# A quarter of each copy of value sums moved from ScalarE to VectorE

## The chip, the core and the metric

The kernel runs on one core of a Trainium2 chip. The metric is the device time of one execution in microseconds; lower is better. The engines are named as in the profile: PE is TensorE's matmul and PEld its weight load, DVE is VectorE, ACT is ScalarE, POOL is GpSimd, and SP is the engine that issues the transfers.

## The reference

For 2048 tokens of width 512, the kernel computes self-attention with 32 heads of 16 and a gated layer of width 1792, and mixes the two by a sigmoid gate per token. All numbers are fp32.

```python
qkv = (x @ wqkv).reshape(B, S, 3, H, Dh)              # H = 32, Dh = 16
scores = einsum("bhqd,bhkd->bhqk", q, k) * Dh ** -0.5
a = (softmax(scores) @ v) @ wo                        # heads side by side
b = (sigmoid(x @ w_gate) * (x @ w_up)) @ w_down       # width F = 1792
g = sigmoid((x * gate_w).sum(-1, keepdims=True))
out = g * a + (1 - g) * b
```

## The kernel before

Attention is done for 16 pairs of heads, one after the other. A loop of 256 steps (`for k in range(NPER)`) holds nearly the whole time: 16 steps a pair, each with two tiles of 128 keys against 1024 queries. A step has five kinds of work, all put in order by hand:

- *Scores and exponentials* (`st_part`, words `t0` and `t1` of the order). TensorE multiplies 512 queries with a tile of keys into a PSUM bank, and ScalarE writes the exponential into a tile `p` (L686). Eight a step.
- *Rows of maxima* (`mx` and `sm_step`, words `m0` and `m1`). The softmax needs the largest score of each query. It is found LEAD steps ahead, from score products of their own (L294), which VectorE reduces from the bank (L296). Eight a step, each of 512 columns.
- *The dense layers* (`dense`, words `d0` and `d1`): halves of matmuls that fill the other half of TensorE's rows; ScalarE takes their sums out of the bank `dn` (L609).
- *Value products* (`values`, at the step's end). 16 matmuls (L848) multiply the step's exponentials with the values and add up in one bank, `sm0`. A copy of 128 x 512 takes the bank into a tile, `sum` for the first of eight steps and `part` for the others.
- *Sums of these copies* (`add`). GpSimd adds each `part` to its `sum`; after eight steps the sum goes to HBM. `part` has two buffers.

The seven banks that scores, maxima and value products share are numbered in `seven`, 0 to 3 for `sm0` to `sm3` and 4 to 6 for `st0` to `st2`. The order of a step says after each word which bank it uses:

```python
STEADY = ("m1:3 t0:2 m0:4 d1 d1 t0:5 m0:6 d1 d1 t0:1 d1 m0:3 d1 t0:2 turn m0:0 t1:4 "
          "m1:5 d0 d0 t1:1 t1:6 d0 d0 m1:2 d0 m1:3 t1:4 d0")
SUMS = 0
```

So the maxima of a step use the banks 3, 4, 6, 3, 0, 5, 2 and 3, in that order, and VectorE reduces them in that order too. The fifth of them uses bank 0, `sm0`, as the value products do: these can start only when VectorE has reduced it. For the last 11 steps (`k >= FREE`) there are no maxima any more, and VectorE does the copy of the value sums; before, ScalarE does it (L853), in 245 steps.

VectorE has other work between the last row of maxima of one step and the first of the next, in some steps: the logit of a token tile (`logits`, L835), reciprocals of the denominators (`dens`, L806), and once in eight steps a reduction and a transpose of the gathered maxima (L300, L302). Each engine takes its instructions in the order written; the order of SP's transfers alone is set by the scheduler.

Of the kernel before, what the change touches and what calls it, by code (L numbers as in the profile page):

```python
# [12 lines left out]
F32 = mybir.dt.float32  # L13
F32R = mybir.dt.float32r
AF = mybir.ActivationFunctionType
# [10 lines left out]
P = 128  # L26
# [9 lines left out]
LEAD = 22  # L36
NSTEP = NPAIR * 32
NPER = NSTEP // 2
FREE = NPER - LEAD // 2
EARLY = 5  # L40
WARM = 9
HF = NF // 2
LOW, UP = 0, 1

# [2 lines left out]
def gated_mix(ctx, tc, x, xT, wqk, wv, wo, w_gate, w_up, w_down, gate_w, out):  # L47
    nc = tc.nc
    pe, act, dve, pool, sp = nc.tensor, nc.scalar, nc.vector, nc.gpsimd, nc.sync

    ctx.enter_context(tc.manual_schedule(engines=ORDERED))
    keep = ctx.enter_context(tc.tile_pool(name="keep", bufs=1))
# [31 lines left out]

    for _ in range(WARM):
        pe.matmul(banks[2], z.to_broadcast([P, P]), z.to_broadcast([P, 512]), start=True, stop=True)
# [33 lines left out]
    def raw_cols(src, n, name):  # L120
        return raw_weights(src[n], [P, KT, P], name)
# [57 lines left out]
    later, turnover, slow, soon = [], [], [], []  # L179
# [210 lines left out]
    def filling():  # L390
        pairs = [(m, i) for i in range(HF) for m in range(2)]
        qk = [(2, 0), (3, 0)]
        jobs = [("qk", 1)] + [("far", i) for i in range(HF + 1)]
        for ns in (qk, pairs):
# [4 lines left out]
        def beside(m, i):  # L399
            return i + HF if m < 2 else i + 1  # L400

        def raws(kind, n):
            if kind == "qk":
                return [raw_qk(n, b) for b in range(2)]
            if kind == "far":
                both = []
                for m in range(2):
                    raw = keep.tile([P, KT, P], F32, name=f"far{m}{n}r", tag="wr", bufs=2)
                    sp.dma_start(raw[:, 2:], gu_w[m][n][:, 2:] if n < HF else wqk[2, 1, :, m])
                    both.append(raw)  # L410
# [6 lines left out]
            if m >= 2:  # L417
                return [raw_weights(wqk[f, :, :, m - 2].rearrange("b p k f -> p b k f"), [P, KT, P],
                                    f"{kind}{m}_{f}") for f in (2, 3)]
            return [raw_cols(gu_w[m], i + a, f"{kind}{m}_{i + a}") for a in (0, HF)]  # L420

# [47 lines left out]
        def out_of(run, name):  # L469
            e = keep.tile([P, 512], F32, name=name, tag="er", bufs=6)  # L470
            leave(e, run.o)
            return e

        def place(m, f, c):
            to = gu_d[m, f] if m < 2 else s_d[m - 2, f]
            return to[:, c * 512:(c + 1) * 512]

        def sums_of(kind, n, ws):
# [7 lines left out]
            elif kind == "far":  # L486
                for m in range(2):
                    for c in range(2):
                        run = Sum(bankd(), quarter(ws[m], 2, c))
                        yield run  # L490
                        sp.dma_start(place(m, n, c) if n < HF else place(2 + m, 0, c), out_of(run, f"far{m}{n}_{c}"))
            elif kind == "side":
# [129 lines left out]
    for c in range(NC):  # L622
# [20 lines left out]
        for i, m in order:  # L643
            o, ops, dst = two[i]
# [167 lines left out]
    def split_load(r):  # L812
        f, t, c = r // 8, r // 4 % 2, r % 4
        e = split_in[r] = keep.tile([P, 2, 512], F32R, name=f"sq{r}", tag="ev", bufs=2)
        sp.dma_start(e[:, 0, :].bitcast(F32), s_d[t, f, :, c * 512:(c + 1) * 512])
# [13 lines left out]
    def logit_load(t):  # L829
        tok[t] = keep.tile([P, 2, D], F32, name=f"xn{t}", tag="ev", bufs=2)  # L830
        sp.dma_start(tok[t], x[t * P:(t + 2) * P, :].rearrange("(t p) d -> p t d", p=P))
# [6 lines left out]
    sums = {}  # L838

    def values(k):  # L840

        o = bank()
        half = divmod(k // 8, 2)
        pts = [ptile.pop((k, b)) for b in range(2)]
        for a in range(2):
            for c in reversed(range(4)):
                h = 2 * half[0] + c // 2
                pe.matmul(o[32 * c:32 * c + VW, :], v[:, 2 * k % 16 + a, h * VW:(h + 1) * VW],  # L848
                          pts[c // 2][:, 2 * a + c % 2, :], start=(a == 0), stop=(a == 1))

        def put(e):
            if 2 * k + LEAD < NSTEP:
                act.activation(e, o, AF.Copy)  # L853
            else:
                dve.tensor_copy(e, o)
        if half not in sums:
            sums[half] = keep.tile([P, 512], F32, name=f"sum{half[0]}_{half[1]}", tag="sum", bufs=2)
            put(sums[half])
        else:
            e = keep.tile([P, 512], F32, name=f"part{k}", tag="part", bufs=2)  # L860
            put(e)
            later.append((1.3, lambda s=sums[half]: add(s, e)))

        def add(s, e):
            pool.tensor_tensor(s, s, e, ALU.add)  # L865
            if k % 8 == 7:
                sp.dma_start(pv_d[half[1], half[0]], s)

    def mx(b):
        for j in range(LEAD, NSTEP):  # L870
            one = sm_step(j)
            for i in range(2):
                one(b, i)
                yield
# [5 lines left out]
    def dense(g):  # L880
        while run:
            run.half(g)
            yield
# [20 lines left out]

    parts = {"m0": mx(0), "m1": mx(1), "d0": dense(LOW), "d1": dense(UP)}
    bank = bankm = lambda: spot[0]
    for k in range(NPER):
        n = 2 * k
        if n + LEAD == NSTEP:
            bank = bank7  # L910
            leave = dve.tensor_copy
        if 75 <= k < 123:
            t, r = divmod(k - 75, 6)
            if r in (0, 3):
                split_load(2 * t + r // 3)
            if r in (1, 4):
                split_sum(2 * t + r // 3)
            if r == 1:
                logit_load(2 * t)
            if r in (3, 4):  # L920
                logits(2 * t, r - 3)
        if n % 32 == 0 and n // 32 + 1 < NPAIR:
            load_pair(n // 32 + 1)
        parts["t0"], parts["t1"] = st_part(k, 0), st_part(k + 1, 1) if k + 1 < NPER else iter(())
        emit(BEGIN if k == 0 else STEADY if k < FREE else LAST, **parts)
        if run and run.done():
            run = next(fill, None)
        elif run and run.n:
            turn(run)
        for half in list(mrow):  # L930
            later[:0] = put_max(half)
        work(2.6)
        later.extend(soon)
        soon.clear()
        if k == NPER - 1:
            break
        if NPER - 16 < k <= NPER - 12:
            for _ in range(2):
                next(next(exps))
        spot[:] = [seven[SUMS]]  # L940
        values(k)
        if k == NPER - 17:
            loaded.extend(hidden_load(*chunks[m]) for m in range(2))
            early = [hidden_early(m) for m in range(2)]
            exps = iter([early[0]] * 4 + [early[1]] * 4)
        if 192 <= k < 215 and k % 8 != 4:
            next(dens[0], None)
        if k == NPER - 6:
            next(dens[1])
        if k == NPER - 2:  # L950
            raws = [late_raw(*late[m][:2]) for m in range(2)]
        if k == NPER - 13:
            early = chain(*early)
        if k >= NPER - 13:
            for _ in range(1 if k < FREE else 3):
                next(early, None)
# [72 lines left out]
    for n, (c, f) in enumerate(chunks):  # L1029
        if f == 0:  # L1030
            down = [bankt() for _ in range(4)]
        if n in at:
            heads_out(at[n], heads.pop(at[n]))
        hl = ready[n]
        for t in range(4):
            ops = list(terms([((hl[0][:, a, t * P:(t + 1) * P], hl[1][:, a, t * P:(t + 1) * P]), wd[f + a])
                              for a in range(2)]))
            for m, (a, b) in enumerate(ops):
                pe.matmul(down[t], a, b, start=(f == 0 and m == 0), stop=(f == NF - 2 and m == 5))  # L1039
            if f == NF - 2:  # L1040
                finish(4 * c + t, down[t], g0)
            if (n, t) == (0, 1):
                values(NPER - 1)
                flush(later)
        if n < 3:
            next(dens[1], None)
        if n in (1, 5, 6, 7):
            next(dens[2], None)
        if n + 3 < len(chunks):
            hidden(n + 3)  # L1050
        if n + 2 < len(chunks):
            hidden_split(n + 2)
        if n + 6 < len(chunks):
            loaded.append(hidden_load(*chunks[n + 6]))
        if n == 1:
            xes.close()
            lp = ctx.enter_context(tc.tile_pool(name="lp", bufs=1))
            wd_h = lp.tile([P, NF - 6, D], F32R, name="wd_h")
            wd_l = lp.tile([P, NF - 6, D], F32R, name="wd_l")
            wohl = keep.tile([P, NS * VROW], F32R, name="wohl", tag="va")[:, :2 * KT * D].rearrange(  # L1060
                "p (a k d) -> p a k d", a=2, k=KT)
        late_next()
        if n + 3 in at:
            u = at[n + 3]
            heads[u] = heads_split(u, *heads[u])
        if n + 5 in at:
            u = at[n + 5]
            heads[u] = heads_load(u)
# [25 lines left out]
```

## Time and profile before

| what | value |
| --- | --- |
| median of 3 runs | 1683.34 us (1683.09 to 1683.47) |
| the profiled execution, its own time | 1682.99 us |
| its span (the basis of the shares) | 1681.0 us |
| TensorE matmul busy | 1675.7 us, 100% |
| VectorE busy | 1453.0 us, 86% |
| ScalarE busy | 1360.9 us, 81% |
| GpSimd busy | 942.5 us, 56% |
| granted TensorE clock | full speed, 9 in all 40 slices |

The span is the time between the first and the last instruction of the program on the core. Busy shares are means over all stages. A matmul row includes the short time that it may wait behind its own weight load, so 100% busy doesn't say that TensorE never waits. A row of the timeline is: start, duration, engine, line, operation, output<-inputs, shapes, number of instructions merged into the row, and in brackets the idle time of the engine before it with what ended it.

### The profile page before, as it was taken

Reading aid. Unit: us, or ns where it says so; the run is one execution under the profiler, and the core shown is the slowest. Engines: PE = TensorE matmul, PEld = TensorE weight load, DVE = VectorE, ACT = ScalarE, POOL = GpSimd, SP = SyncE. Lnnn points to the kernel's source line nnn. Section 1 sums busy time; section 2 is a strip of 40 time slices with the busy share of each in tenths; the row PEclk is TensorE's granted clock in tenths of the full one; section 3 lists DMA queues with packets and bytes.
Section 4 is the critical chain, followed back from the end, with each engine's and each line's share of the span. In section 5 each row is a group of like instructions: output and inputs, shape, how many; then the busy total and the mean of one; then the engine's idle time right before and its main releaser. Section 6 shows DMA issues by size and latency. Waiting matters only on the chain.

```text
span 1681.0 us, 34649 instructions
## 1 busy us (share of the span) xinstructions
PE 1675.7 (100%) x12485; PEld 1060.1 (63%) x12485; DVE 1453.0 (86%) x2350; ACT 1360.9 (81%) x2656; POOL 942.5 (56%) x922
## 2 busy tenths in 40 slices
PE   9999999999999999999999999999999999999999
PEld 7766656565656565656565665656565656568887
DVE  7988888888889999999888888889999888887753
ACT  4188888898988898889898989889898989983431
POOL 1134476547656666566666767676666667653110
PEclk9999999999999999999999999999999999999999
DMA  8411447366565564555535353434343434368862
GB/s 271 119 46 59 130 171 211 133 171 206 145 198 136 164 151 154 160 166 188 160 103 146 102 146 108 134 103 133 109 134 105 133 114 158 123 206 277 288 217 70
DMA packets 143788, 254.20 MB, mean 151 GB/s; under 512 B 24256, under 2 KB 36544, under 8 KB 140736
## 3 DMA queue, kind: packets, MB, share of 16 engines
q1 hardware_dynamic: 135024, 235.34, 46.3%
q10 hardware_dynamic: 8592, 16.65, 3.1%
q8 instruction: 98, 1.61, 0.4%
q14 instruction: 74, 0.61, 0.1%
HBM read 149.42 MB, written 102.50 MB: 150 GB/s over the span
## 4 chain that ended last, share of the span: by engine, by line
PE 99%; DVE 0%; DMA 0%; ACT 0%; ACTq 0%; issue 0%; DVEq 0%
PE dn L163 30%; PE sm L848 27%; PE sm L294 16%; PE sm L1039 5%; PE st L684 5%; PE sm L684 5%; PE st L294 2%; PE dn L1039 2%; PE st L1039 2%; PE st L163 2%; PE st L150 1%; PE st L646 1%; PE sm L150 1%; PE st L848 1%; DVE stat L296 0%; DMA x<-in_xT_dram 0%
## 5 line engine op out<-in xcount | busy, mean ns | idle before, releaser
L296 DVE TENSOR_REDUCE stat<-sm 128x1 f32<-128x512 f32 x1314 | 848.2, 681 | 136.6 <-PE sm L684 125.8
L686 ACT ACTIVATE p<-sm 128x512 f32<-128x512 f32 x1030 | 611.0, 630 | 11.3 <-PE st L163 10.1
L686 ACT ACTIVATE p<-st 128x512 f32<-128x512 f32 x1018 | 615.6, 651 | 0.0
L294 PE MATMUL sm<-ks,qs 48*128 48x512 f32 x1314 | 525.2, 435 | 0.0
L848 PE MATMUL sm<-p,v 128*17 128x512 f32 x4016 | 479.9, 595 | 0.0
L296 DVE TENSOR_REDUCE stat<-st 128x1 f32<-128x512 f32 x734 | 478.8, 680 | 0.0
L684 PE MATMUL sm<-qs,ks 64*128 64x512 f32 x1030 | 428.6, 419 | 0.0
L684 PE MATMUL st<-qs,ks 64*128 64x512 f32 x1018 | 425.5, 419 | 0.0
L294 PEld LDWEIGHTS sm<-ks,qs 48*128 48x128 f32 x1314 | 241.0, 184 | 261.7 <-DVE stat L296 214.9
L865 POOL TENSOR_TENSOR sum<-sum,part 128x512 f32<-128x512 f32 x224 | 288.6, 1288 | 135.5 <-PE sm L684 121.7
L294 PE MATMUL st<-ks,qs 48*128 48x512 f32 x734 | 290.0, 395 | 0.0
L848 PEld LDWEIGHTS sm<-p,v 128*17 128x17 f32 x4016 | 93.1, 96 | 224.3 <-issue 155.4
L853 ACT ACTIVATE part<-sm 128x512 f32<-128x512 f32 x214 | 128.3, 600 | 124.1 <-issue 84.1
L544 POOL TENSOR_TENSOR chain<-chain,chain 128x512 f32<-128x512 f32 x96 | 124.3, 1294 | 155.4 <-PE sm L684 140.4
L684 PEld LDWEIGHTS st<-qs,ks 64*128 64x128 f32 x1018 | 187.3, 184 | 29.6 <-issue 3.4
L684 PEld LDWEIGHTS sm<-qs,ks 64*128 64x128 f32 x1030 | 190.0, 185 | 10.5 <-issue 5.1
L544 POOL TENSOR_TENSOR had<-chain,had 128x512 f32<-128x512 f32 x96 | 123.6, 1287 | 39.4 <-PE sm L684 17.8
L294 PEld LDWEIGHTS st<-ks,qs 48*128 48x128 f32 x734 | 137.0, 187 | 1.5 <-ACT v L667 0.5
L609 ACT ACTIVATE chain<-dn 128x512 f32<-128x512 f32 x128 | 88.2, 689 | 0.0
L544 POOL TENSOR_TENSOR side<-side,side 128x512 f32<-128x512 f32 x32 | 41.4, 1294 | 77.9 <-PE sm L684 71.9
L105 POOL TENSOR_TENSOR ol<-ot,oh 128x512 fp32r<-128x512 f32 (+1 forms) x8 | 14.7, 1842 | 102.7 <-ACT oh L102 81.5
L321 POOL CAST mhl<-mt 128x32 fp32r<-128x32 f32 x32 | 7.6, 238 | 101.0 <-DVE mt L302 101.0
(912 smaller groups left out, 3251.5 us busy)
## 6 DMA issues: line engine op xcount, KB each, us to landing
gul<-gu_d SPq DMA_DIRECT2D x56, 512.0 KB
had<-gu_d SPq DMA_DIRECT2D x84, 256.0 KB
gu_d<-had SPq DMA_DIRECT2D x84, 256.0 KB
gu_d<-side SPq DMA_DIRECT2D x56, 256.0 KB
pv_d<-sum SPq DMA_DIRECT2D x32, 256.0 KB
qs<-q_d SPq DMA_DIRECT2D x30, 256.0 KB
ks<-k_d SPq DMA_DIRECT2D x30, 256.0 KB
gu_d<-far SPq DMA_DIRECT2D x28, 256.0 KB
```

What stands on the lines that cost most here:

```text
L150: pe.matmul(o, a, b, start=(i == 0), stop=(i == len(ops) - 1))
L163: mm = pe.matmul(self.o, a[rows], b[rows], start=(self.n == 0), stop=(self.n == 2 * len(self.ops) - 1))
L294: pe.matmul(t, qs[r:r + KM, qt * P:(qt + 1) * P], ks[r:r + KM, g * 512:(g + 1) * 512], start=True, stop=True)
L296: dve.tensor_reduce(stat[half][:, b, qt % 8, g:g + 1], t, axis=AX.X, op=ALU.max)
L544: pool.tensor_tensor(to, u, w, ALU.add)
L609: leave = lambda e, o: act.activation(e, o, AF.Copy)
L684: pe.matmul(o, ks[r:r + KR, (kt + a) * P:(kt + a + 1) * P], qs[r:r + KR, q0:q0 + 512], start=True, stop=True)
L686: act.activation(pt[:, 2 * a + c, :], o, AF.Exp, scale=DH ** -0.5)
L848: pe.matmul(o[32 * c:32 * c + VW, :], v[:, 2 * k % 16 + a, h * VW:(h + 1) * VW], pts[c // 2][:, 2 * a + c % 2, :], start=(a == 0), stop=(a ...
L853: act.activation(e, o, AF.Copy)
L865: pool.tensor_tensor(s, s, e, ALU.add)
L1039: pe.matmul(down[t], a, b, start=(f == 0 and m == 0), stop=(f == NF - 2 and m == 5))
```

## The change

In each step before FREE, the copy of the value sums is divided by columns: ScalarE copies the first 384 (`SHARE`), VectorE the other 128. In steps in which VectorE has a logit or a reciprocal to do in that place, and in the last ones before FREE (`busy`), ScalarE still copies all 512. `values` now returns the function that does the copy, and the loop calls it at the start of the next step, behind VectorE's other work of the step and ahead of the first row of maxima of the next.

```diff
+SHARE = 384
 ...
         def put(e):
-            if 2 * k + LEAD < NSTEP:
-                act.activation(e, o, AF.Copy)
+            if k >= FREE:
+                dve.tensor_copy(e, o)
+                return
+            n = 512 if busy(k) else SHARE
+            act.activation(e[:, :n], o[:, :n], AF.Copy)
+            if n < 512:
+                dve.tensor_copy(e[:, n:], o[:, n:])
+
+        def leave_sums():
+            if half not in sums:
+                sums[half] = keep.tile([P, 512], F32, name=f"sum{half[0]}_{half[1]}", tag="sum", bufs=2)
+                put(sums[half])
             else:
-                dve.tensor_copy(e, o)
-        if half not in sums:
-            sums[half] = keep.tile([P, 512], F32, name=f"sum{half[0]}_{half[1]}", tag="sum", bufs=2)
-            put(sums[half])
-        else:
-            e = keep.tile([P, 512], F32, name=f"part{k}", tag="part", bufs=2)
-            put(e)
-            later.append((1.3, lambda s=sums[half]: add(s, e)))
+                e = keep.tile([P, 512], F32, name=f"part{k}", tag="part", bufs=2)
+                put(e)
+                later.append((1.3, lambda s=sums[half]: add(s, e)))
 ...
+        return leave_sums
+
+    def busy(k):
+
+        return (78 <= k + 1 < 123 and (k + 1 - 75) % 6 in (3, 4)) or (192 <= k < 215 and k % 8 != 4) or k >= NPER - 13
 ...
+    leaving = []
     for k in range(NPER):
         n = 2 * k
+        while leaving:
+            leaving.pop()()
 ...
-        values(k)
+        leaving.append(values(k))
+        if k >= FREE:
+            leaving.pop()()
 ...
-                values(NPER - 1)
+                values(NPER - 1)()
```

What the change does to the order shows on three engines. The names are those of the tiles with their numbers, which differ between the two programs; what stands in brackets are the counts of other engines that the instruction waits for. On VectorE, at the end of step 62, before (the last row of maxima of the step and the first of the next both read bank `sm3`, and are the two in the row with x2):

```order
L296 TENSOR_REDUCE stat4_1_5151<-sm0_69 128x1 [waits PE_49]
L296 TENSOR_REDUCE stat4_1_5151<-st1_66 128x1 [waits PE_49]
L296 TENSOR_REDUCE stat4_1_5151<-sm2_71 128x1 [waits PE_49]
L296 TENSOR_REDUCE stat4_1_5151<-sm3_72 128x1 [waits PE_49] x2
L296 TENSOR_REDUCE stat4_1_5151<-st0_65 128x1 [waits PE_49]
L296 TENSOR_REDUCE stat4_1_5151<-st2_67 128x1 [waits PE_49]
```

and in the changed program, at the same place:

```order
L297 TENSOR_REDUCE stat4_1_5212<-sm0_69 128x1 [waits PE_49]
L297 TENSOR_REDUCE stat4_1_5212<-st1_66 128x1 [waits PE_49]
L297 TENSOR_REDUCE stat4_1_5212<-sm2_71 128x1 [waits PE_49]
L297 TENSOR_REDUCE stat4_1_5212<-sm3_72 128x1 [waits PE_49]
L859 COPY part62_5339<-sm0_69 128x128 [waits Activation_49]
L297 TENSOR_REDUCE stat4_1_5212<-sm3_72 128x1 [waits PE_49]
L297 TENSOR_REDUCE stat4_1_5212<-st0_65 128x1 [waits PE_49]
L297 TENSOR_REDUCE stat4_1_5212<-st2_67 128x1 [waits PE_49]
```

The copy stands between the two rows of maxima that were neighbours, and it waits for ScalarE's count (Activation), not for TensorE's. The program has 207 such copies; the count that each waits for is the one that ScalarE's copy of the same step sets.

On ScalarE, around the same copy, before:

```order
L686 ACTIVATE p63_1_5245<-st0_65 128x512 [waits PE_49]
L609 ACTIVATE chain20_12_5266<-dn_68 128x512 [waits PE_49]
L853 ACTIVATE part62_5277<-sm0_69 128x512 [waits DVE_49,PE_49,Pool_49]
L686 ACTIVATE p63_0_5281<-sm2_71 128x512 [waits PE_49,Activation_49]
L686 ACTIVATE p63_0_5281<-st1_66 128x512 [waits PE_49]
```

and after:

```order
L687 ACTIVATE p63_1_5307<-st0_65 128x512 [waits PE_49]
L610 ACTIVATE chain20_12_5328<-dn_68 128x512 [waits PE_49]
L857 ACTIVATE part62_5339<-sm0_69 128x384 [waits DVE_49,PE_49,Pool_49]
L687 ACTIVATE p63_0_5344<-sm2_71 128x512 [waits PE_49,Activation_49]
L687 ACTIVATE p63_0_5344<-st1_66 128x512 [waits PE_49]
```

ScalarE's copy has kept its place and its waits, and has 384 columns. On POOL, the sum that takes this copy in, with the one ahead of it and three neighbours, before:

```order
L865 TENSOR_TENSOR sum3_1_4880<-sum3_1_4880,part61_5214 128x512 [waits Activation_49]
L544 TENSOR_TENSOR chain20_12_5266<-chain20_12_5266,chain20_11_5202 128x512 [waits PE_49,Activation_49]
L544 TENSOR_TENSOR had20_12_5204<-chain20_12_5266,had20_12_5204 128x512 [waits DMAHW3_49,DMAHW2_49,Pool_49]
L865 TENSOR_TENSOR sum3_1_4880<-sum3_1_4880,part62_5277 128x512 [waits Activation_49]
L544 TENSOR_TENSOR chain20_13_5329<-chain20_13_5329,chain20_12_5266 128x512 [waits PE_49,Activation_49]
```

and after:

```order
L871 TENSOR_TENSOR sum3_1_4936<-sum3_1_4936,part61_5275 128x512 [waits DVE_49]
L545 TENSOR_TENSOR chain20_12_5328<-chain20_12_5328,chain20_11_5263 128x512 [waits PE_49,Activation_49]
L545 TENSOR_TENSOR had20_12_5265<-chain20_12_5328,had20_12_5265 128x512 [waits DMAHW3_49,DMAHW2_49,Pool_49]
L871 TENSOR_TENSOR sum3_1_4936<-sum3_1_4936,part62_5339 128x512 [waits DVE_49]
L545 TENSOR_TENSOR chain20_13_5392<-chain20_13_5392,chain20_12_5328 128x512 [waits PE_49,Activation_49]
```

The sum waits for VectorE's count instead of ScalarE's. TensorE's order is the same, and SP's has three transfers (two stores of `side`, one of `had`) a place or a few away from where they were.

## The prediction

> **What bounds the kernel now.** I read the page's busy shares first, then the chain that ended last, then the list of waits, and last one step of the long middle stretch in order of time.
>
> ```profile
> PE 1675.7 (100%) x12485; PEld 1060.1 (63%) x12485; DVE 1453.0 (86%) x2350; ACT 1360.9 (81%) x2656; POOL 942.5 (56%) x922
> ...
> PE 99%; DVE 0%; DMA 0%; ACT 0%; ACTq 0%; issue 0%; DVEq 0%
> ```
>
> TensorE seems to be everything, but a busy matmul row includes short stalls, and both lines average over the program. The waits say more:
>
> ```profile
> PEld sm L294 <- DVE stat L296: 214.9, 278, 0.9
> DVE stat L296 <- PE sm L684: 125.8, 187, 0.9
> PEld sm L848 <- DVE stat L296: 66.0, 244, 0.4
> PEld sm L848 <- ACT p L686: 2.9, 9, 0.4
> ```
>
> Columns are total us, times, longest. TensorE's weight loads wait for VectorE's maxima (L296) once for the value products (L848) in 244 steps, and VectorE waits for TensorE about once a step. TensorE hardly waits for ScalarE's exponentials (9 times). So TensorE and VectorE hand work to each other in a loop, and ScalarE stands beside it. One step, rows of TensorE, VectorE and ScalarE:
>
> ```profile
> 703.57 1.91 PE L848 MATMUL sm<-p,v 128*17 128x512 f32 x16
> ...
> 705.41 0.50 PE L294 MATMUL sm<-ks,qs 48*128 48x512 f32 x1
> ...
> 705.60 0.60 ACT L853 ACTIVATE part<-sm 128x512 f32<-128x512 f32 x1 [0.57 <-POOL side_12r L450]
> ...
> 705.95 0.69 DVE L296 TENSOR_REDUCE stat<-sm 128x1 f32<-128x512 f32 x1 [0.71 <-PE sm L684]
> 706.55 1.28 DVE L296 TENSOR_REDUCE stat<-st 128x1 f32<-128x512 f32 x2
> 707.75 1.28 DVE L296 TENSOR_REDUCE stat<-sm 128x1 f32<-128x512 f32 x2
> ...
> 709.15 1.91 PE L848 MATMUL sm<-p,v 128*17 128x512 f32 x16
> 709.54 1.28 DVE L296 TENSOR_REDUCE stat<-sm 128x1 f32<-128x512 f32 x2
> ```
>
> A step, from one value product to the next, is 709.15 - 703.57 = 5.58 us. The value products write bank sm0 from 703.57; when they are through, TensorE issues the step's first maxima matmul (705.41) and ScalarE copies sm0 out (705.60 to 706.20). VectorE, idle for 0.71 us, takes its first row of maxima at 705.95. Five rows follow without a gap, start to start 0.60 though one lasts 0.69 and two take 1.28; the fifth, which reads sm0, ends at 707.75 + 1.28 = 709.03, and 0.12 later the next value products start. So the loop is: value products and first maxima matmul 2.38, five maxima 3.08, hand-over 0.12. Three more maxima (the last two in the last row) end at 710.82, inside the next products. VectorE's 0.71 us of idle time is real, but whatever starts the row at 705.95 later makes the step longer.
>
> The trace has a test of that. In some steps VectorE does a token's logit (L835) in the same gap, and one of them took 1.29 us:
>
> ```profile
> 518.21 1.91 PE L848 MATMUL sm<-p,v 128*17 128x512 f32 x16
> ...
> 519.80 1.29 DVE L835 CUSTOM_DVE_ANT_0 xn<-xn,gwb 128x512 f32<-128x512 f32 x1
> ...
> 521.02 0.68 DVE L296 TENSOR_REDUCE stat<-sm 128x1 f32<-128x512 f32 x1
> ...
> 524.22 1.05 PE L848 MATMUL sm<-p,v 128*17 128x512 f32 x8
> ```
>
> The first row of maxima stood at 521.02 - 518.21 = 2.81 instead of 2.38, 0.43 late; the step took 524.22 - 518.21 = 6.01 instead of 5.58, 0.43 longer. Lateness there is passed on in full.
>
> **The change part by part.** Of the 245 copies that ScalarE makes now, 207 are divided, 384 columns to ScalarE and 128 to VectorE; 38 stay whole (`busy`). Of the last 11 steps nothing changes: VectorE copies there now.
>
> *ScalarE's shorter copy.* It stays in its place in ScalarE's order. Rows for its price, and for VectorE's:
>
> ```profile
> L853 ACT ACTIVATE part<-sm 128x512 f32<-128x512 f32 x214 | 128.3, 600 | 124.1 <-issue 84.1 <-PE sm L848 9.6 <-POOL mh L358 2.9
> ...
> L102 ACT ACTIVATE hl<-gul 128x1024 fp32r<-128x1024 f32 x26 | 27.4, 1052 | 13.6 <-DVE gul L766 10.5 <-PE sm L1039 3.1
> ...
> L102 ACT ACTIVATE xh<-x 128x512 fp32r<-128x512 f32 x15 | 8.3, 624 | 1.6 <-DMA x<-in_xT_dram 1.6
> ...
> L300 DVE TENSOR_REDUCE mpad<-stat 128x16 f32<-128x64 f32 x32 | 7.0, 220 | 1.2
> ```
>
> ScalarE's copies take 1052 ns for 1024 columns and 624 for 512, 0.84 ns a column, so 128 columns fewer save 107 ns: 600 becomes 493. That by itself is worth nothing: ScalarE is not in the loop (it sat idle 0.57 us before its copy in the step above), and its exponentials only come 0.1 earlier.
>
> *VectorE's part, and the wait it brings.* The changed program's VectorE copy waits for one thing, ScalarE's count, at the value that ScalarE's copy of the same step sets. So the two do not share the time; they stand one behind the other. No row of before has VectorE following ScalarE in this place. The nearest is the start of the program, where VectorE reads the bank that ScalarE has just read:
>
> ```profile
> 16.52 0.60 ACT L228 ACTIVATE qe<-st 128x512 fp32r<-128x512 f32 x1 [2.01 <-PE st L646]
> ...
> 17.16 0.69 DVE L229 TENSOR_TENSOR qe<-st,qe 128x512 fp32r<-128x512 f32 x1 [1.24 <-ACT qe L228]
> ```
>
> From ScalarE's end (17.12) to VectorE's start is 0.03 to 0.04. So in the step shown the copy would start at 705.60 + 0.49 + 0.03 = 706.12, when the first maxima matmul has long been done. Its length: VectorE takes 220 ns for 64 columns (L300) and 0.68 us for 512 (the maxima above), 1.03 ns a column, so 286 for 128. The next maxima may start 0.08 before its end, as the maxima do among themselves (0.69 and 0.68 long, 0.60 apart): 706.12 + 0.29 - 0.08 = 706.33, against 705.95 now. That is 0.38 late, in 207 steps 79 us. Queued behind the waiting copy on VectorE is that row of maxima; behind it, TensorE's second use of bank sm3, the other four maxima, and the next value products. None of this has slack, as the logit step shows.
>
> The bounds of this term. The copy can't well be shorter than the 64-column row (220 ns): 0.31 a step, 64 us. If the next maxima waited for the copy's very end, the 0.08 is gone: 0.46 a step, 95 us. I take 0.38, since 128 columns lie near the short row and every pair of maxima shows the overlap.
>
> The Trainium skill has a rule on that overlap: "VectorE: DVE Perf Modes", section "The DRAIN you can't avoid", says that the next operation doesn't start until the pipe is empty. By it the step would lose the 0.46; the rows here, 0.60 apart at 0.68 long, speak for 0.38.
>
> *GpSimd's sum* (L865, now L871) waits for VectorE's copy instead of ScalarE's, which ends at 706.41 instead of 706.20. In the step shown it starts at 707.48, more than a microsecond later, so it costs nothing. If POOL were that close behind, it would pay 0.2. *The bank:* sm0 is written again by the fifth maxima matmul, which started at 707.27 in the step shown, 0.86 after the copy's end: nothing. *SP's queue:* the same transfers, three of them a place earlier or later: nothing, as the chain has 0% DMA. *TensorE's order* is the same.
>
> ```profile
> 707.27 0.40 PE L294 MATMUL sm<-ks,qs 48*128 48x512 f32 x1
> ...
> 707.48 1.29 POOL L865 TENSOR_TENSOR sum<-sum,part 128x512 f32<-128x512 f32 x1 [1.03 <-PE sm L684]
> ```
>
> The sum: +79 us on the profiled execution's 1682.99 (span 1681.0), which is 0.35 under the median of the runs; so 1683.3 + 79 = 1762.
>
> **The rivals.** *Hidden in the gap, no change: 1683.* If the two engines read the bank side by side, VectorE's copy would run from about 705.60 to 705.89 and the maxima start at 705.95 as now. The gap of 0.71 speaks for it. It decides at this point: the copy has to start by 705.95 + 0.08 - 0.29 = 705.74, and ScalarE's part, which it waits for, ends at 706.09. The wait in the program's order is against it. The Trainium skill agrees, in "PSUM — Partial Sum Buffer", section "PSUM bank collisions raise a hardware error": two engines may not access one bank in the same partitions at once, two reads included. By that rule no order that keeps the two in one bank can use the gap, and the sum is 79; without it, 0. No run here shows such a collision.
>
> *Faster: 1661.* If ScalarE set the step, 107 ns less would take 207 x 0.107 = 22 us off. Against it: 9 waits on its exponentials, 2.9 us in all, and its idle 0.57 a step.
>
> *The full drain: 1778.* The next maxima wait for the end of the copy, 0.46 a step, as above.
>
> *The change is not made in most steps:* then 1683. The program has 207 of these copies, so I give this nothing.
>
> **How the numbers follow.** A step's loss between 0.31 and 0.46, mostly near 0.38: 88 in 100, with 1762 as its time. Full drain: 5. Hidden: 4. Faster: 2. The last 1 is a larger loss from something not seen. The range goes from the 64-column price, 1683 + 64 = 1747, to the full drain, 1683 + 95 = 1778; it leaves out under 10 in 100, and unless a bound is wrong no narrower end can be argued. Slower by over 0.2% (3.4 us, about what a measurement of this kernel can tell): 94; within: 4; faster: 2.
>
> **What would show it.** Right: value products 5.95 to 5.97 apart in the 207 steps and 5.58 in the others; VectorE's 128-column copy 0.03 after ScalarE's end, about 0.29 long, its idle time before it ended by ScalarE; the first maxima 2.76 behind the value products instead of 2.38; ScalarE's copy at 0.49. Wrong: a VectorE copy that starts before ScalarE's has ended (the hidden case); a step that stays at 5.58 although the first maxima are late, which would mean slack among the five that I don't see; or steps over 6.1, which would mean a second wait, of POOL or ScalarE, that the longer step lets in.

## The result, and the profile after

The changed kernel takes 1766.05 us (median of 4 runs, 1764.8 to 1766.43) against 1683.4: ratio 1.0487, 95% interval 1.0469 to 1.0506. The forecast was 1762 with a range of 1747 to 1778. The profiled execution has a span of 1764.3 us, 83.3 more than before. Its page and its list of waits, to be read beside those of before:

```profile
PE 1753.2 (99%) x12485; PEld 1041.2 (59%) x12485; DVE 1495.9 (85%) x2557; ACT 1374.1 (78%) x2656; POOL 942.8 (53%) x922
```

```profile
PEld sm L295 <- DVE stat L297: 303.7, 483, 3.4
...
DVE part L859 <- ACT part L857: 148.2, 181, 3.9
...
PEld sm L849 <- DVE stat L297: 85.0, 244, 0.7
```

The new wait is in the second list as forecast: VectorE's copy (L859) waits for ScalarE's (L857) in all 181 steps with a `part`; another 26 with a `sum` have a row of their own. TensorE's waits for VectorE grew, from 214.9 to 303.7 us for the maxima's weights. The two copies by shape (mean ns is the number before the second bar):

```profile
L857 ACT ACTIVATE part<-sm 128x384 f32<-128x384 f32 x181 | 89.1, 492 | 125.1 <-issue 76.3 <-PE sm L849 11.0 <-POOL mh L359 4.6
...
L859 DVE COPY part<-sm 128x128 f32<-128x128 f32 x181 | 52.8, 292 | 148.2 <-ACT part L857 148.2
```

One step, value product to value product, as it was shown of before:

```profile
934.05 1.91 PE L849 MATMUL sm<-p,v 128*17 128x512 f32 x16
...
935.89 0.50 PE L295 MATMUL sm<-ks,qs 48*128 48x512 f32 x1
...
936.08 0.49 ACT L857 ACTIVATE part<-sm 128x384 f32<-128x384 f32 x1 [0.66 <-issue]
...
936.60 0.29 DVE L859 COPY part<-sm 128x128 f32<-128x128 f32 x1 [0.87 <-ACT part L857]
936.81 0.68 DVE L297 TENSOR_REDUCE stat<-sm 128x1 f32<-128x512 f32 x1
937.41 1.28 DVE L297 TENSOR_REDUCE stat<-st 128x1 f32<-128x512 f32 x2
938.61 1.28 DVE L297 TENSOR_REDUCE stat<-sm 128x1 f32<-128x512 f32 x2
...
940.00 1.05 PE L849 MATMUL sm<-p,v 128*17 128x512 f32 x8
```

The first maxima's matmul is through by 936.39, but VectorE takes that row only at 936.81: 2.76 behind the value products instead of 2.38. Behind five rows of maxima (the fifth ends at 939.89) the next products start at 940.00, a step of 5.95 instead of 5.58.

### The profile page after: what moved, and what is told of

Read it like the earlier page. It is cut to its first block, busy times and chain, and to the rows that moved or that the text cites. A ratio compares the mean times of both kernels' runs of the same rounds, so it can differ in the third digit from the quotient of the medians.

```text
span 1764.3 us, 34850 instructions
## 1 busy us (share of the span) xinstructions
PE 1753.2 (99%) x12485; PEld 1041.2 (59%) x12485; DVE 1495.9 (85%) x2557; ACT 1374.1 (78%) x2656; POOL 942.8 (53%) x922
## 4 chain that ended last, share of the span: by engine, by line
PE 97%; DMA 1%; DVE 1%; POOL 0%; ACT 0%; issue 0%; ACTq 0%; DVEq 0%; POOLq 0%; SPq 0%
PE sm L849 26%; PE dn L164 25%; PE sm L295 19%; PE sm L685 6%; PE st L685 5%; PE sm L1055 5%; PE st L295 3%; PE dn L1055 2%; PE st L164 2%; PE st L1055 2%; PE st L151 1%; PE sm L151 1%; PE st L849 1%; DVE stat L297 0%; DMA wv_r<-in_wv_dram 0%; DMA qs<-q_d 0%
## 5 line engine op out<-in xcount | busy, mean ns | idle before, releaser
L687 ACT ACTIVATE p<-sm 128x512 f32<-128x512 f32 x1030 | 622.3, 613 | 55.7 <-PE sm L685 54.8
L687 ACT ACTIVATE p<-st 128x512 f32<-128x512 f32 x1018 | 593.4, 619 | 0.7 <-PE st L685 0.5
L295 PEld LDWEIGHTS sm<-ks,qs 48*128 48x128 f32 x1314 | 241.3, 184 | 338.4 <-DVE stat L297 303.7
L857 ACT ACTIVATE part<-sm 128x384 f32<-128x384 f32 (+1 forms) x214 | 108.8, 509 | 144.5 <-issue 89.0
L859 DVE COPY part<-sm 128x128 f32<-128x128 f32 x181 | 52.8, 292 | 148.2 <-ACT part L857 148.2
L610 ACT ACTIVATE chain<-dn 128x512 f32<-128x512 f32 x128 | 83.0, 648 | 0.0
```

What stands on the lines that cost most here:

```text
L295: pe.matmul(t, qs[r:r + KM, qt * P:(qt + 1) * P], ks[r:r + KM, g * 512:(g + 1) * 512], start=True, stop=True)
L610: leave = lambda e, o: act.activation(e, o, AF.Copy)
L687: act.activation(pt[:, 2 * a + c, :], o, AF.Exp, scale=DH ** -0.5)
L857: act.activation(e[:, :n], o[:, :n], AF.Copy)
L859: dve.tensor_copy(e[:, n:], o[:, n:])
```

## The experiments

Eight kernels were run. Where a table gives a step, it is the median over the first 244 steps of that kernel's trace, and "first maxima" and "first exponential" are the starts of VectorE's first row and of ScalarE's first exponential, counted from the start of the value products before them.

### Fewer columns on VectorE

```diff
-SHARE = 384
+SHARE = 480
```

> The changed kernel with 32 columns on VectorE instead of 128 (480 on ScalarE). Theory: the two copies stand one behind the other, so what VectorE no longer copies ScalarE copies. ScalarE's part 0.573 us, VectorE's 0.19, first maxima at 2.03 + 0.573 + 0.032 + 0.19 - 0.084 = 2.74 behind the value products, 0.36 late; in 207 steps 75 us: 1757 to 1763, against 1766 with 128 columns. Rival 1 (VectorE's work is the loss, in proportion to its columns): a quarter of the 83 us, or with the fixed part of a short copy (0.19 of 0.29) some 54 us: 1704 to 1737.

Measured: 1761.66 us, ratio to before 1.0466 (1.0452 to 1.0481). With a quarter of VectorE's columns left, only 4 us of the 83 are gone. The two rows of its trace say why:

```profile
L857 ACT ACTIVATE part<-sm 128x480 f32<-128x480 f32 x181 | 103.6, 572 | 125.1 <-issue 76.1 <-PE sm L849 11.0 <-POOL mh L359 4.6
...
L859 DVE COPY part<-sm 128x32 f32<-128x32 f32 x181 | 34.7, 192 | 163.1 <-ACT part L857 163.1
```

ScalarE's part is 80 ns longer, VectorE's 100 shorter; one stands behind the other, so the sum falls by 20 ns only. The first maxima came at 2.74, as worked out. Rival 1 is wrong here by some 25 us.

### The two parts exchanged

```diff
             n = 512 if busy(k) else SHARE
-            act.activation(e[:, :n], o[:, :n], AF.Copy)
             if n < 512:
                 dve.tensor_copy(e[:, n:], o[:, n:])
+            if n:
+                act.activation(e[:, :n], o[:, :n], AF.Copy)
```

> In the changed kernel the two parts of the copy are exchanged: VectorE takes its 128 columns first and ScalarE's 384 wait for VectorE; places in both queues are the same. Theory (the loss is VectorE's wait for ScalarE, which moves the first row of maxima from 2.38 to 2.76 us behind the value products): VectorE's copy starts as soon as the products are done, at about 1.98, is 0.29 long, and the first maxima stay at 2.38; ScalarE's part moves from 2.03 to about 2.30, which its idle 0.57 us hides. Step 5.58 us, time 1680 to 1687. Rival 1 (VectorE's added work itself is the loss, wherever it stands: 0.21 to 0.29 us in 207 steps): 1726 to 1743. Rival 2 (ScalarE's shorter copy is worth 0.107 us a step once nothing hides it): about 1661.

Measured: 1727.56 us, ratio 1.0265 (1.0251 to 1.0279). That is the number of rival 1, and my expectation missed. But the trace shows VectorE's copy and its first maxima within 0.07 us of where the theory had put them, and the step longer all the same:

```profile
909.06 1.91 PE L849 MATMUL sm<-p,v 128*17 128x512 f32 x16
...
911.11 0.29 DVE L858 COPY part<-sm 128x128 f32<-128x128 f32 x1 [0.59 <-PE sm L849]
911.43 0.69 DVE L297 TENSOR_REDUCE stat<-sm 128x1 f32<-128x512 f32 x1
...
911.43 0.49 ACT L860 ACTIVATE part<-sm 128x384 f32<-128x384 f32 x1 [0.90 <-DVE part L858]
911.82 0.59 ACT L687 ACTIVATE p<-sm 128x512 f32<-128x512 f32 x1
...
913.24 1.28 DVE L297 TENSOR_REDUCE stat<-sm 128x1 f32<-128x512 f32 x2
...
914.42 0.18 PEld L685 LDWEIGHTS st<-qs,ks 64*128 64x128 f32 x1 [0.19 <-ACT p L687]
...
914.85 1.48 PE L849 MATMUL sm<-p,v 128*17 128x512 f32 x12
```

The first maxima are at 911.43, 2.37 behind the products, and the fifth ends at 914.52. The products could follow 0.12 later; they start at 914.85. The last score matmul ahead of them was held (row 914.42) by an exponential of ScalarE, whose bank it needs. ScalarE's first exponential is at 2.76 here, against 2.52 before. The list of waits has this as a pair of rows that were 0.5 and 0.6 us before, and VectorE holds the value products in 66 steps instead of 244:

```profile
PEld sm L849 <- DVE stat L297: 17.6, 66, 0.4
...
PEld st L685 <- ACT p L687: 40.9, 210, 0.2
PEld sm L685 <- ACT p L687: 40.8, 213, 0.2
```

So ScalarE has a loop of its own: value products, copy, exponentials, the scores that reuse their banks, value products. It is 0.57 us idle in it before each copy, and still has next to no room, because that idle time is the value products' own. New theory: a step ends at the later of two times, 3.19 behind the first maxima (VectorE's loop) and about 3.04 behind the first exponential (ScalarE's). Before, these are 2.38 + 3.19 = 5.57 and 2.52 + 3.04 = 5.56, so there is almost nothing between them. The trace of before has a step that shows the second loop, the 46th (steps are counted from 0):

```profile
345.20 1.91 PE L848 MATMUL sm<-p,v 128*17 128x512 f32 x16
...
347.58 0.69 DVE L296 TENSOR_REDUCE stat<-sm 128x1 f32<-128x512 f32 x1 [0.71 <-PE sm L684]
...
347.95 0.60 ACT L686 ACTIVATE p<-sm 128x512 f32<-128x512 f32 x1
...
350.56 0.18 PEld L684 LDWEIGHTS st<-qs,ks 64*128 64x128 f32 x1 [0.20 <-ACT p L686]
...
350.99 1.91 PE L848 MATMUL sm<-p,v 128*17 128x512 f32 x16
```

The first maxima are on time at 2.38, the first exponential is late at 2.75, and the step takes 5.79 = 2.75 + 3.04. Rival 1 gives the same time for the exchanged parts as the two loops do, so the next kernel tells them apart.

### VectorE's quarter alone

```diff
             n = 512 if busy(k) else SHARE
-            act.activation(e[:, :n], o[:, :n], AF.Copy)
             if n < 512:
+                pool.memset(e[:, :n], 1.0)
                 dve.tensor_copy(e[:, n:], o[:, n:])
+            else:
+                act.activation(e, o, AF.Copy)
```

> VectorE copies its 128 columns in the 207 steps and ScalarE nothing; the other 384 columns are not taken from the bank but filled with ones by GpSimd, so three quarters of the value sums of these steps are left out. VectorE's added work is all there, in the same place, and nobody waits one behind the other. Theory (waiting is the loss, not work): VectorE's copy starts 2.05 behind the value products, ends at 2.34, first maxima at 2.38 as before; ScalarE's first exponential at 2.47 or earlier instead of 2.52; step 5.57, time 1680 to 1685. Rival 1 (VectorE's added work is the loss, which gave the number that was measured with the two parts exchanged, 1727.6): 1726 to 1743.

Measured: 1685.4 us, ratio 1.0012 (1.0003 to 1.0021). VectorE's step:

```profile
885.34 0.29 DVE L859 COPY part<-sm 128x128 f32<-128x128 f32 x1 [0.37 <-PE sm L849]
885.67 0.69 DVE L297 TENSOR_REDUCE stat<-sm 128x1 f32<-128x512 f32 x1
```

The value products of this step start at 883.30; the copy stands at 2.04 and the first maxima at 2.37, as before. All of VectorE's added work is in the gap and costs at most 2 us of the 83. Its median step is 5.573, that of before; the rest lies in a few long steps. In the longest, of 6.61, VectorE is not what holds it: ScalarE's first exponential came at 3.57, behind a load that its queue issued late (such loads are the subject of the last experiment), and 3.57 + 3.04 is 6.61. The others were not looked into. Rival 1 is out.

### ScalarE's shorter copy alone

```diff
             if n < 512:
-                dve.tensor_copy(e[:, n:], o[:, n:])
+                pool.memset(e[:, n:], 1.0)
```

> ScalarE copies 384 columns and VectorE none; the other 128 columns of each copy are not taken from the bank but filled with ones by GpSimd, so this leaves a quarter of the value sums out. It shows ScalarE's shorter copy by itself. Theory: ScalarE is not in the loop, the step stays at 5.58 us: 1680 to 1687. Rival 2 (ScalarE sets the step): 0.107 us less in 207 steps, about 1661.

Measured: 1683.76 us, ratio 1.0005 (0.9996 to 1.0013). Rival 2 is out: ScalarE's first exponential comes at 2.47 instead of 2.52, and VectorE's loop holds the step at 5.57. The saving is 0.05 and not 0.107, since that exponential now meets the end of its score matmul: with no copy on ScalarE at all (VectorE's quarter alone) it waits for that matmul in the trace, and comes at 2.47 too.

### The whole copy on VectorE

The order of the exchanged parts, with no columns for ScalarE in the 207 steps:

```diff
-SHARE = 384
+SHARE = 0
```

> VectorE copies all 512 columns in the 207 steps, ScalarE none. With the two parts exchanged the first maxima stood at 2.38 as before and the step was still 0.22 longer: ScalarE's first exponential came 0.24 late, at 2.76, and the scores that wait for ScalarE's banks with it. Theory of two loops (value products 3.19 behind the first maxima, and 3.04 behind the first exponential, whichever is later): VectorE's copy from 2.05 to 2.74, first maxima at 2.66, exponential at 2.47, step 2.66 + 3.19 = 5.85; 0.28 in 207 steps are 57 us: 1735 to 1746. Rival (only ScalarE's loop is tight, VectorE's has room): 1683 or less.

Measured: 1738.7 us, ratio 1.0332 (1.0316 to 1.0348).

```profile
917.12 0.69 DVE L858 COPY part<-sm 128x512 f32<-128x512 f32 x1 [0.37 <-PE sm L849]
917.73 0.68 DVE L297 TENSOR_REDUCE stat<-sm 128x1 f32<-128x512 f32 x1
```

The products of this step start at 915.08: first maxima at 2.65, where 2.66 was worked out, and a median step of 5.85. VectorE's loop has no room beyond the gap, while ScalarE, without a copy, has some to spare. It is quicker than the changed kernel by 27 us, some 23 of them since no part waits for another and 4 since the changed kernel's longest step (the last experiment) is short here; it is no gain over before.

### Both loops, one at a time and together

```diff
+            seen = t[:, :480] if b == 0 and j >= LEAD else t
-            dve.tensor_reduce(stat[half][:, b, qt % 8, g:g + 1], t, axis=AX.X, op=ALU.max)
+            dve.tensor_reduce(stat[half][:, b, qt % 8, g:g + 1], seen, axis=AX.X, op=ALU.max)
```

> The kernel before, with 480 instead of 512 columns read in four of the eight rows of maxima of a step (those of the first head of a pair, which are the second to the fifth that VectorE takes); 32 of 512 keys are left out of these maxima. VectorE's loop is shortened by 4 x 32 x 1.04 ns = 0.13 us, ScalarE's is as before. Theory of two loops: ScalarE's, 2.52 + 3.03 to 3.05 = 5.55 to 5.57, holds the step: 1677 to 1684. Rival (VectorE's loop alone sets the step): 5.44, in 244 steps 32 us off: about 1651.

Measured: 1676.42 us, ratio 0.9959 (0.9947 to 0.9972); the median step is 5.558. The rival's 1651 is out. The time is 0.6 us under the expected range. Steps that were long before, those with a late logit (6.01, 5.88, 5.92, 5.88), take 5.56, 5.70, 5.55 and 5.68 here; without that gain of 1.2 the time would lie in the range. What holds the step now is in these rows:

```profile
881.48 1.21 DVE L297 TENSOR_REDUCE stat<-sm 128x1 f32<-128x480 f32 x2
...
881.79 0.65 ACT L687 ACTIVATE p<-st 128x512 f32<-128x512 f32 x1
...
882.49 0.18 PEld L685 LDWEIGHTS st<-qs,ks 64*128 64x128 f32 x1
...
882.92 0.12 PEld L849 LDWEIGHTS sm<-p,v 128*17 128x17 f32 x6 [0.25 <-DVE stat L297]
```

The list names VectorE as the releaser of the value products. But its fifth row of maxima ended at 881.48 + 1.21 = 882.69, 0.23 earlier, where it was 0.12 before. The last score's weights were loaded at 882.49, 0.05 after the exponential that frees its bank (882.44). The same trace has both lengths of ScalarE's loop: 209 steps with the first exponential at 2.52 take 5.56, and 34 with it at 2.47 take 5.52.

> Both at once: the short maxima, and ScalarE's copy of 384 columns in 207 steps with the other 128 filled with ones by GpSimd (both leave out part of the computation, as told of each). Theory of two loops: VectorE's 5.44, ScalarE's 2.47 + 3.04 = 5.51, so the step falls to about 5.51 where neither change alone moved it: 0.05 to 0.07 in 207 steps, 10 to 15 us: 1667 to 1674. Rival (TensorE's own matmuls hold the step at 5.57, whatever the other two do): 1680 to 1685.

This kernel has the edits of the short maxima and of ScalarE's shorter copy. Measured: 1672.16 us, ratio 0.9933 (0.9921 to 0.9946), step 5.53, first exponential 2.47: 2.47 + 3.04 = 5.51 was worked out. ScalarE's shorter copy, worth nothing by itself, takes 4 us off once VectorE's loop is shorter. So it is not TensorE's own work that holds the step at 5.57.

The two loops against the traces follow (with the short maxima, VectorE's loop is 3.06 instead of 3.19: four rows shorter by 32 columns at 1.04 ns). The 3.19 was read from the kernel before and the 3.04 from the exchanged parts, so these two rows fit by construction; VectorE whole, maxima short and both short were forecast with them.

| kernel | first maxima + 3.19 | first exponential + 3.04 | step |
| --- | --- | --- | --- |
| before | 2.38 + 3.19 = 5.57 | 2.52 + 3.04 = 5.56 | 5.57 |
| changed | 2.76 + 3.19 = 5.95 | 2.47 + 3.04 = 5.51 | 5.95 |
| 32 columns | 2.74 + 3.19 = 5.93 | 2.50 + 3.04 = 5.54 | 5.92 |
| exchanged | 2.38 + 3.19 = 5.57 | 2.76 + 3.04 = 5.80 | 5.79 |
| VectorE whole | 2.66 + 3.19 = 5.85 | 2.47 + 3.04 = 5.51 | 5.85 |
| ScalarE short | 2.38 + 3.19 = 5.57 | 2.47 + 3.04 = 5.51 | 5.57 |
| maxima short | 2.38 + 3.06 = 5.44 | 2.52 + 3.04 = 5.56 | 5.56 |
| both short | 2.38 + 3.06 = 5.44 | 2.47 + 3.04 = 5.51 | 5.53 |

### The 4 us above the forecast

In the changed kernel one step, the 127th, took 9.92 us. ScalarE's and VectorE's rows in it:

```profile
840.35 0.37 ACTq L379 DMA_DIRECT2D xh<-t_d  x1
...
844.67 0.37 ACTq L379 DMA_DIRECT2D xl<-t_d  x1
845.16 0.49 ACT L857 ACTIVATE part<-sm 128x384 f32<-128x384 f32 x1 [3.65 <-DMA qs<-q_d]
...
845.68 0.29 DVE L859 COPY part<-sm 128x128 f32<-128x128 f32 x1 [3.85 <-ACT part L857]
```

ScalarE's queue also issues loads. The second of two (ACTq) went out 4.3 us after the first, and the copy stood behind it; VectorE's copy and the maxima stood behind that. Before, the same two loads went out 0.4 us apart. The bracket at the copy names what ended the wait, the landing of a `qs` load: the second load waits for a semaphore that a `qs` load issued by SP at 837.37 had used before it, whose last packet landed at 844.65, and the load went out at 844.67. The wait itself makes 2.97 of the step's extra 3.97 (its first maxima come at 5.73). The rest, and the 0.48 by which the next step is long, go with the clock: TensorE had been idle for 2.98 us, and from 847.76 to 851.17 the granted clock was 0.5. The test:

```diff
-            act.dma_start(xs[:, k0:k0 + 2, cols].bitcast(F32), t_d[n, a, c].rearrange("k p s -> p k s"))
+            sp.dma_start(xs[:, k0:k0 + 2, cols].bitcast(F32), t_d[n, a, c].rearrange("k p s -> p k s"))
```

> The changed kernel with the 28 loads of xh and xl out of t_d issued by SP instead of ScalarE. In the changed kernel's profile one step (the 127th) took 9.92 us: a load on ScalarE's queue was issued 4.3 us after the one ahead of it, ScalarE's copy came 3 us late, and VectorE's copy and the maxima behind it. Theory: this is the 4 us by which the measured 1766 lies above the forecast 1762, and it comes from VectorE now waiting for whatever holds ScalarE: 1760 to 1763. Rival (the 4 us are many small losses in other steps, or the step is long for another reason): 1765 to 1768.

Measured: 1762.51 us (1761.02 to 1764.52), ratio 1.0475 (1.0459 to 1.0491). In the trace, of a run of 1761.33, the 127th step is 5.95 again, the long step behind it (6.43) is gone, and the granted clock is full from 4.8 us to the last 3 us of the program. So the load on ScalarE's queue made the two long steps, which are 4.45 us together. Three steps of 6.23 elsewhere, in which that queue issued no load, are gone too, and one of 6.23 is new; these were not explained. The time is not settled as well as the trace: two of the four runs, at 1763.69 and 1764.52, have a mean granted clock of 0.999, while the other two have 1.000 and the changed kernel's four 0.998 or 0.999, so something like the long step may have come up in them; their traces were not taken. Why the `qs` load took 7.3 us to land was not tried.

## Why the prediction was right

*The sum.* Its terms, per step, forecast and measured: ScalarE's part 493 ns and 492; hand-over 0.03 and 0.032; VectorE's part 286 and 292; overlap with the next maxima 0.08 and 0.084; first maxima late by 0.38 and 0.38 (2.76 against 2.38); passed on in full, 5.945 against 5.573 in the median step. 207 times 0.37 is 77 us. With a few long steps that gives the 83 of the span, and without the 127th and the one behind it 79, the forecast.

*The wait that wasn't in the trace.* The order of the changed program named it, and a pair of rows at the start of the kernel priced it. That the copies stand one behind the other, and not that VectorE has more to do, is shown by the 32 columns (nearly the same loss for a quarter of the columns) and by VectorE's quarter alone (the same work on VectorE for 2 us).

*The overlap.* VectorE's rows stayed 0.08 into each other after a copy too, so the full drain (1778) did not come about here. The Trainium skill, in "VectorE: DVE Perf Modes", section "The DRAIN you can't avoid", says more than the prediction took from it: a next operation that is not held starts earlier than the empty pipe. The 0.08 agrees with that.

*GpSimd, the bank and SP* were costed at nothing. GpSimd's busy time is the same (942.8 against 942.5). SP and ScalarE's queue were not nothing: the step of 9.92 us is a term that the prediction did not have. It had asked only whether the transfers land in time, and not who issues them and what stands behind that. Steps over 6.1 were the prediction's own sign of a second wait, and six of the 244 are: the two of the held load, three of 6.23 that were not explained, and one of 6.22 in which VectorE has a row of 1.53 us (L779) ahead of its maxima.

*Where it was wrong without harm.* "That by itself is worth nothing: ScalarE is not in the loop." The first half is shown. The second is not so: ScalarE is in a second loop with about 0.01 us to spare, and its 0.57 us of idle time is no room at all. In the changed kernel this does not show, as VectorE's loop is 0.4 longer than ScalarE's. With the parts exchanged it does, and the same misreading made that expectation miss by 41 us. The forecast's price for "faster", 22 us, was too high as well: the first exponential can come only 0.05 earlier. And the sentence that no order which keeps the two in one bank can use the gap was wrong: with the parts exchanged VectorE's copy lay in the gap, and the first maxima stayed at 2.37.

*Side by side was not tried*, so what two reads of one bank at once would do stays open here.

## What to carry to other kernels

Dividing a copy out of one bank between two engines did not halve it: the parts ran one behind the other, and the second engine inherited the first one's lateness, its queue's included. Ask of each engine's idle time what ends it: time spent waiting for a step of the same loop is not room, and here two loops of nearly the same length stood in one step, of which the list of waits named only one. Shortening one of two such loops shows little, and lengthening either shows in full, so a trial should move each of them alone before work is shifted between them.

## What the runs showed of the hardware

A copy's time on VectorE was 192 ns for 32 columns, 292 for 128 and 685 to 692 for 512, and on ScalarE 492, 572 and 599 for 384, 480 and 512. At the 1.04 ns a column that lie between VectorE's first two, some 160 of the 192 ns do not depend on the columns. From ScalarE's end to VectorE's start took 32 ns in the median step. A load held in ScalarE's queue kept ScalarE's compute back for 3.65 us, until the transfer that had last used its semaphore had landed. Soon after 2.98 us in which TensorE stood idle, the granted clock was 0.5 for 3.41 us (3.13 and 3.41 with 32 columns); what made it fall was not tried.
